# Rescaling of 64-bit weights on GpSimd without the absolute value, and the squares of that stage on ScalarE

## The chip, the cores and the metric

One core of one Trainium2 chip. The metric is the device time of one launch in microseconds; the kernel before has a median of 714.84 us over three runs (712.4 to 716.45).

## The reference

Three layers follow each other. Attention between 4 x 8 sequences of 512 rows and 32 state rows, both ways; a dense layer of 512 x 2048 x 512 on the resulting 2176 tokens with g = h * tanh(softplus(h)); a layer of 8 experts, of which each token takes the one with the largest similarity.

```python
scores = scale * np.matmul(x, state.transpose(0, 1, 3, 2))
a = np.exp(scores - scores.max(-1, keepdims=True)); a /= a.sum(-1, keepdims=True) + 1e-09
xread = np.matmul(a, state)
...
h = x @ w_in
sp = np.where(h > 20.0, h, np.log1p(np.exp(np.minimum(h, 20.0))))
g = h * np.tanh(sp)
return (g @ w_out).astype(np.float32)
```

The weights `w_in` and `w_out` arrive as 64-bit floats, seen by the kernel as pairs of 32-bit words.

## The kernel before

**Conversion.** The two weights are 32 tiles of 128 x 512 (16 of `w_in`, 16 of `w_out`; `order0`, line 197: the first 8 of each, then the second 8). `load_w` loads one raw tile of 512 KB into one of two buffers (`raw`); `convert_w` calls `convert` (line 87) on it. The high word, read as a 32-bit float and rescaled, has the wanted exponent three bits too low: line 96 rescales it with an absolute value on ScalarE into `x`, line 99 makes three more mantissa bits of the low word on GpSimd, and VectorE puts them together in two instructions (lines 100 and 101, both recorded at line 70): shift left by three and or, then or with the sign bit of the raw tile. The second of them frees the raw buffer for the next load. `split` (line 72) then makes a rounded copy on ScalarE (line 73, `wih`, `woh`) and the rest on GpSimd (line 74, `wil`, `wol`). Names carry the tile: `wc05x` is tile 5 of `w_in`, `wc115x` tile 15 of `w_out`.

**Steps.** The dense layer runs in steps (chunk of 512 tokens, slice of 128 of the 2048 hidden values), listed in `steps` from `RUNS`: steps 0 to 7 are slices 0 to 7 of chunk 0, steps 8 to 23 slices 0 to 15 of chunk 1. `l1` makes the hidden slice in PSUM (`h`), `mish_a` (line 508) makes tanh and silu of it on ScalarE (lines 513 and 514, the start of a step there) and squares the tanh in `z` (tile `er`): line 517 on ScalarE or line 519 on VectorE. `mish_b` makes two more squares on ScalarE (lines 542, 543) and two products on VectorE (line 70). `g_split` splits the result (`gh` on ScalarE, `gl` on VectorE), and `l2` multiplies it with `w_out`, two steps later. In the first 24 steps (`NCONV`) each step also calls `convert_w` at its end.

**Attention.** Ahead of the steps, eight units go through four phases; GpSimd subtracts the maximum (line 372) and applies the reciprocal sum (line 387). The first 8 conversions are called among them, two more before step 2; steps 0 and 1 begin during its last units.

**What sets the order.** Outside the last chunk the order of instructions on each engine is made at build time by a scheduler with its own model of costs, so a change of one instruction's engine can move its neighbours too. Each engine then executes its list in order.

Of the kernel before, what the change touches and what calls it, by code (L numbers as in the profile page):

```python
# [8 lines left out]
F32 = mybir.dt.float32  # L9
# [6 lines left out]
ALU = mybir.AluOpType  # L16
AF = mybir.ActivationFunctionType
# [20 lines left out]
NCONV = 24  # L38
# [13 lines left out]
def body(tc, x, state, w_in, w_out, ee, tau, w1, w2, out):  # L52
    nc = tc.nc
    T, V, A, G, Y = nc.tensor, nc.vector, nc.scalar, nc.gpsimd, nc.sync
# [14 lines left out]
    def stt(o, a, s, b, op0, op1):  # L69
        V.scalar_tensor_tensor(out=o, in0=a, scalar=s, in1=b, op0=op0, op1=op1)  # L70

    def split(hi, lo, src, eng=None):
        A.activation(hi, src, AF.Copy)  # L73
        (eng or V).tensor_tensor(out=lo, in0=src, in1=hi.bitcast(F32), op=ALU.subtract)  # L74
# [12 lines left out]
    def convert(pl, hi, lo, raw, name, bufs):  # L87

        if not wide:
            split(hi, lo, raw[:, 0:512], G)  # L90
            return
        low, top = raw[:, :, 0], raw[:, :, 1]
        x = pl.tile([P, 512], U32, tag="cx", name=name + "x", bufs=bufs)
        xf = x.bitcast(F32)

        A.activation(xf, top.bitcast(F32), AF.Abs, scale=2.0**-112)

        l16 = raw.rearrange("p a b -> p (a b)").bitcast(U16).rearrange("p (a b) -> p a b", b=4)[:, :, 1]
        G.tensor_scalar(out=low, in0=l16, scalar1=2.0**-13, scalar2=-0.49994, op0=ALU.mult, op1=ALU.add)
        stt(x, x, 3, low, ALU.logical_shift_left, ALU.bitwise_or)  # L100
        stt(x, top, 0x80000000, x, ALU.bitwise_and, ALU.bitwise_or)
        split(hi, lo, xf, G)
# [6 lines left out]
    with stack:  # L109
# [82 lines left out]
        def pair(name):  # L192
            t = mt.tile([P, 2, 512], F32, tag="er", bufs=2, name=name)
            return t[:, 0, :], t[:, 1, :]
# [14 lines left out]
        def convert_w():  # L209
            o, i = j = order.pop(0)  # L210
            if o:
                hi, lo = (w[i // 2][:, i % 2, :] for w in (WOH, WOL))
            else:
                g, k = divmod(i, KT)
                hi, lo = (w[g // 2][k][:, g % 2 * 512 : (g % 2 + 1) * 512] for w in (WIH, WIL))
            convert(cv, hi, lo, raws.pop(j), f"wc{o}{i}", 2)
            load_w()
# [290 lines left out]
        def mish_a(c, f):  # L508

            z, _ = pair(f"er{c}_{f}")  # L510
            u = mt.tile([P, 512], F32, tag="u", bufs=2, name=f"u{c}_{f}")
            h = hps.pop((c, f))
            A.activation(z, h, AF.Tanh, scale=0.5, bias=mb_[:, 0:1])  # L513
            A.activation(u, h, AF.Silu)  # L514

            if steps.index((c, f)) < NCONV and f % 2:
                A.activation(z, z, AF.Square)
            else:
                V.tensor_tensor(out=z, in0=z, in1=z, op=ALU.mult)  # L519

            nrm[c, f] = u, z, h
# [532 lines left out]
        steps = [(c, f) for c, a, b in RUNS for f in range(a, b)]  # L1054
# [43 lines left out]
        def start(g):  # L1098
            l1(*steps[g])
            following(*steps[g])  # L1100
            mish_a(*steps[g])
            if g:
                finish(g - 1)
            mish_b(*steps[g])
# [66 lines left out]
        for g, (c, f) in enumerate(steps):  # L1171
# [32 lines left out]
            if at == 2 and r:  # L1204
                pc, pf, _ = RUNS[r - 1]
                evac(pc, pf)
                if 1 < r < len(RUNS) - 2:
                    todo += [ab(pc, i) for i in range(CHUNKS[pc][1] + 2)]
            mish_a(c, f)
            if c != LC or f:  # L1210
                finish(g - 1)
# [113 lines left out]
```

## Time and profile before

| | |
|---|---|
| median of three runs | 714.84 us (712.4 to 716.45) |
| the profiled execution | 714.88 us, of which the span is 713.0 us |
| mean granted TensorE clock | 0.987 of full |
| busy: TensorE, VectorE, ScalarE, GpSimd | 670.7, 479.5, 453.4, 188.1 us |

Rows below are of that execution; times in them count from the start of the span. PE is TensorE, PEld its weight loads, DVE VectorE, ACT ScalarE, POOL GpSimd, SP SyncE. L96 is line 96 of the kernel before.

### The profile page before, as it was taken

The numbers are of one execution on the slowest core, as the hardware profiler recorded it, in microseconds if no ns is written. First come the engines' busy times: TensorE is split into PE (matmuls) and PEld (weight loads), VectorE is DVE, ScalarE is ACT, GpSimd is POOL, SyncE is SP. The second block draws the span as 40 slices with busy tenths as digits, with TensorE's granted clock in tenths as the row PEclk, the third lists the DMA queues.
The fourth block names the chain that finished last, engine by engine and source line by source line (L and its number), as shares of the span: only waits on it lengthen the run. The fifth ranks groups of instructions, "written<-read, shape, count | busy, mean of one in ns | idle before, by whom it ended". The sixth has DMA issues, their size and how long they took to land.

```text
span 713.0 us, 11919 instructions
## 1 busy us (share of the span) xinstructions
PE 670.7 (94%) x3517; PEld 550.4 (77%) x3517; DVE 479.5 (67%) x1002; ACT 453.4 (64%) x798; POOL 188.1 (26%) x166
## 2 busy tenths in 40 slices
PE   8888998999999999999999889999999999999894
PEld 8788876778888888888887768877876788777673
DVE  5977798989477776776679687673345751347751
ACT  5876989989798677677776687314334641246640
POOL 2785355562000030210030454021211211121101
PEclk9999999999999999999999989999999999999997
DMA  7662143430010454422021656014416641257440
GB/s 196 151 172 90 60 127 110 148 118 31 1 60 0 123 112 99 89 56 86 29 75 61 207 192 213 10 60 148 161 50 221 220 133 61 95 205 242 190 136 18
DMA packets 57829, 81.23 MB, mean 114 GB/s; under 512 B 24970, under 2 KB 35722, under 8 KB 57748
## 3 DMA queue, kind: packets, MB, share of 16 engines
q1 hardware_dynamic: 54388, 70.31, 32.5%
q0 software_dynamic: 3360, 9.99, 4.3%
q8 instruction: 33, 0.54, 0.3%
q14 instruction: 48, 0.39, 0.2%
HBM read 64.00 MB, written 13.65 MB: 109 GB/s over the span
## 4 chain that ended last, share of the span: by engine, by line
PE 42%; issue 24%; DMA 13%; ACT 9%; DVE 8%; POOL 3%; SPq 0%; POOLq 0%; DVEq 0%; ACTq 0%
DMA out<-ys,ix 8%; PE acc L105 6%; PE acc L106 6%; PE acc L107 6%; PE h L105 3%; PE h L106 3%; PE h L107 3%; DMA es<-in_moe_w 2%; PE lg L599 2%; DMA w<-in_moe_w_out 2%; DMA w<-in_moe_w_in 1%; ACT er L513 1%; PE x1t L588 1%; PE hp L107 1%; PE hp L106 1%
## 5 line engine op out<-in xcount | busy, mean ns | idle before, releaser
L105 PE MATMUL acc<-woh,gh 128*128 128x512 f32 x272 | 109.8, 407 | 5.5 <-ACT gh L73 5.5
L106 PE MATMUL acc<-wol,gh 128*128 128x512 f32 x272 | 108.3, 399 | 0.0
L107 PE MATMUL acc<-woh,gl 128*128 128x512 f32 x272 | 94.2, 402 | 1.0 <-DVE gl L74 0.9
L1051 POOL DMA_INDIRECT out<-ys,ix x21 | 21.2, 1011 | 203.4 <-DVEq L1048 108.8
L105 PEld LDWEIGHTS acc<-woh,gh 128*128 128x128 f32 x272 | 51.8, 191 | 18.8 <-ACT gh L73 8.6
L107 PEld LDWEIGHTS acc<-woh,gl 128*128 128x128 f32 x272 | 51.0, 190 | 14.5 <-DVE gl L74 3.3
L513 ACT ACTIVATE er<-h,mb__104 128x512 f32<-128x512 f32 x68 | 46.8, 688 | 23.8 <-PE h L107 21.6
L106 PEld LDWEIGHTS acc<-wol,gh 128*128 128x128 f32 x272 | 51.8, 190 | 10.3
L985 PE MATMUL y<-w2h,hth 128*128 128x512 f32 x136 | 55.9, 411 | 2.8 <-DVE htl L74 1.1
L519 DVE TENSOR_TENSOR er<-er 128x512 f32<-128x512 f32 x56 | 41.3, 737 | 23.1 <-ACT er L513 22.7
L985 PE MATMUL hp<-w1h,xth 128*128 128x512 f32 x136 | 55.3, 407 | 0.8 <-PE ht L1020 0.2
L986 PE MATMUL y<-w2l,hth 128*128 128x512 f32 x136 | 55.2, 406 | 0.1
L986 PE MATMUL hp<-w1l,xth 128*128 128x512 f32 x136 | 53.8, 395 | 0.0
L105 PE MATMUL h<-xh,mh 128*128 128x512 f32 x128 | 52.0, 406 | 0.5 <-ACT xh L73 0.5
L542 ACT ACTIVATE h<-er,mb__104 128x512 f32<-128x512 f32 x68 | 47.4, 697 | 7.3 <-DVE er L519 4.9
L106 PE MATMUL h<-xl,mh 128*128 128x512 f32 x128 | 50.9, 397 | 0.4 <-DVE xl L74 0.4
L107 PE MATMUL h<-xh,ml 128*128 128x512 f32 x128 | 50.5, 395 | 0.0
L543 ACT ACTIVATE er<-er,mb__104 128x512 f32<-128x512 f32 x68 | 49.5, 727 | 1.2
L73 ACT ACTIVATE xth<-gt 128x512 fp32r<-128x512 f32 (+1 forms) x21 | 11.4, 543 | 57.7 <-PE gt L965 57.7
L73 ACT ACTIVATE hth<-ht 128x512 fp32r<-128x512 f32 x32 | 17.5, 595 | 42.3 <-PE ht L1020 40.9
L62 DVE TENSOR_SCALAR ys<-y,gt 128x512 f32<-128x512 f32 x21 | 15.7, 748 | 39.1 <-PE y L990 32.1
L514 ACT ACTIVATE u<-h 128x512 f32<-128x512 f32 x68 | 40.6, 597 | 0.0
(456 smaller groups left out, 1717.6 us busy)
## 6 DMA issues: line engine op xcount, KB each, us to landing
sg<-in_moe_w SPq DMA_DIRECT2D x48, 512.0 KB, 5.2
w<-in_moe_w_in SPq DMA_DIRECT2D x16, 512.0 KB, 4.1
w<-in_moe_w_out SPq DMA_DIRECT2D x16, 512.0 KB, 3.3
es<-in_moe_w SPq DMA_DIRECT2D x32, 256.0 KB, 3.0
xn<-in_x SPq DMA_DIRECT2D x32, 128.0 KB, 3.4
md<-mr SPq DMA_DIRECT2D x28, 128.0 KB, 2.5
x1d<-x SPq DMA_DIRECT2D x13, 256.0 KB, 3.2
mh<-mr SPq DMA_DIRECT2D x28, 64.0 KB, 2.1
```

The costliest lines, as they stand in the source:

```text
L73: A.activation(hi, src, AF.Copy)
L105: T.matmul(o, lh, rh, start=first, stop=False)
L106: T.matmul(o, lh, rl, start=False, stop=False)
L107: T.matmul(o, ll, rh, start=False, stop=last)
L513: A.activation(z, h, AF.Tanh, scale=0.5, bias=mb_[:, 0:1])
L514: A.activation(u, h, AF.Silu)
L519: V.tensor_tensor(out=z, in0=z, in1=z, op=ALU.mult)
L542: A.activation(r, z, AF.Square, scale=QS, bias=mb_[:, 1:2])
L543: A.activation(z, z, AF.Square, scale=QS, bias=mb_[:, 2:3])
L985: T.matmul(o, h, wh, start=k == 0, stop=False)
L986: T.matmul(o, h, wl, start=False, stop=k == len(terms) - 1)
L1051: G.indirect_dma_start(out=out[:, :], out_offset=bass.IndirectOffsetOnAxis(ap=ix, axis=0), in_=y, in_offset=None, bounds_check=NTOK - 1, o ...
```

## The change

Line 96 goes from ScalarE to GpSimd as a plain multiplication that keeps the sign; the shift left by three in the next instruction drops the sign bit together with two exponent bits, so the absolute value is not needed. In the first 24 steps the square of every step is done on ScalarE (line 517), where before the even slices had theirs on VectorE (line 519).

```diff
-        A.activation(xf, top.bitcast(F32), AF.Abs, scale=2.0**-112)
+        G.tensor_scalar(out=xf, in0=top.bitcast(F32), scalar1=2.0**-112, scalar2=None, op0=ALU.mult)
...
-            if steps.index((c, f)) < NCONV and f % 2:
+            if steps.index((c, f)) < NCONV:
                 A.activation(z, z, AF.Square)
             else:
                 V.tensor_tensor(out=z, in0=z, in1=z, op=ALU.mult)
```

The order on the engines moves at more places than these. On GpSimd, at the end of the attention stage, before (`w_...` is a raw tile, `a_...` a unit's weights):

```order
L372 TENSOR_TENSOR a_876<-ss_789,mx_874 128x512
L74 TENSOR_TENSOR wil_178<-wc07x,wih_170 128x512
L99 TENSOR_SCALAR w_988<-w_988 128x512
L99 TENSOR_SCALAR w_1122<-w_1122 128x512
L387 TENSOR_TENSOR a_876<-a_876,sm_890 128x512
L372 TENSOR_TENSOR a_934<-ss_872,mx_932 128x512
L99 TENSOR_SCALAR w_1131<-w_1131 128x512
L387 TENSOR_TENSOR a_934<-a_934,sm_948 128x512
```

And with the change:

```order
L372 TENSOR_TENSOR a_934<-ss_872,mx_932 128x512
L387 TENSOR_TENSOR a_876<-a_876,sm_890 128x512
L96 TENSOR_SCALAR wc07x<-w_847 128x512
L74 TENSOR_TENSOR wil_177<-wc06x,wih_169 128x512
L99 TENSOR_SCALAR w_930<-w_930 128x512
L387 TENSOR_TENSOR a_934<-a_934,sm_948 128x512
L96 TENSOR_SCALAR wc10x<-w_930 128x512
L74 TENSOR_TENSOR wil_178<-wc07x,wih_170 128x512
L99 TENSOR_SCALAR w_988<-w_988 128x512
L96 TENSOR_SCALAR wc11x<-w_988 128x512
L99 TENSOR_SCALAR w_1122<-w_1122 128x512
```

Three of line 99 (`w_988`, `w_1122`, `w_1131`) and one split moved behind the last unit's line 387.

On VectorE, at the end of the conversion, before (`h_9` is slice 9 of chunk 1, step 17):

```order
L74 TENSOR_TENSOR gl_8_1933<-h_8_1850,gh_8_1932 128x512
L70 SCALAR_TENSOR_TENSOR wc115x<-wc115x,w_2149 128x512
L70 SCALAR_TENSOR_TENSOR wc115x<-w_2149,wc115x 128x512
L70 SCALAR_TENSOR_TENSOR h_9_1908<-h_9_1908,u_9_1928 128x512
L519 TENSOR_TENSOR er_10_1985<-er_10_1985 128x512
```

And with the change:

```order
L74 TENSOR_TENSOR gl_10_2032<-h_10_1949,gh_10_2031 128x512
L70 SCALAR_TENSOR_TENSOR wc115x<-wc115x,w_2149 128x512
L70 SCALAR_TENSOR_TENSOR wc115x<-w_2149,wc115x 128x512
L70 SCALAR_TENSOR_TENSOR h_11_2007<-h_11_2007,u_11_2027 128x512
L70 SCALAR_TENSOR_TENSOR h_11_2007<-er_11_2026,h_11_2007 128x512
```

The last conversion stands two steps later, and line 519 is gone from these steps.

## Rows read from the trace of the kernel before

**Rows 1.** The page, part 1: busy time of each engine.

```profile
PE 670.7 (94%) x3517; PEld 550.4 (77%) x3517; DVE 479.5 (67%) x1002; ACT 453.4 (64%) x798; POOL 188.1 (26%) x166
```

**Rows 2.** Windows by stage: us, busy time and instructions by engine, clock, DMA.

```profile
16.00:62.00 46.00, 37.97 (x327) 36.03 (x328) 40.77 (x98) 35.06 (x72) 35.00 (x30) 1.00 0.57 162
...
100.00:166.00 66.00, 60.95 (x286) 47.26 (x285) 59.31 (x84) 60.42 (x110) 37.61 (x34) 1.00 0.39 125
166.00:200.00 34.00, 34.00 (x160) 28.05 (x159) 21.72 (x34) 26.45 (x46) 3.10 (x3) 1.00 0.00 1
...
78.94:174.47 95.53, 90.48 (x427) 71.80 (x426) 86.08 (x124) 88.25 (x161) 51.86 (x45) 1.00 0.35 111
```

**Rows 3.** Timeline of ACT, line 513, steps 2, 18, 20, 21: start, duration.

```profile
78.94 0.67 ACT L513 ACTIVATE er<-h,mb__104 128x512 f32<-128x512 f32 x1
...
165.26 0.72 ACT L513 ACTIVATE er<-h,mb__104 128x512 f32<-128x512 f32 x1
...
174.47 0.69 ACT L513 ACTIVATE er<-h,mb__104 128x512 f32<-128x512 f32 x1 [0.25 <-PE h L107]
178.66 0.69 ACT L513 ACTIVATE er<-h,mb__104 128x512 f32<-128x512 f32 x1 [1.19 <-PE h L107]
```

**Rows 4.** Waits, 100 to 165 us: total, times, longest.

```profile
PEld acc L105 <- ACT gh L73: 6.6, 7, 2.2
POOL w L99 <- DMA w<-in_moe_w_in: 6.4, 5, 1.7
POOL w L99 <- DMA w<-in_moe_w_out: 5.4, 5, 1.2
...
PE acc L105 <- ACT gh L73: 3.9, 5, 1.7
```

**Rows 5.** Timeline of ACT: conversions 12 and 32, and instructions with their followers.

```profile
80.67 0.68 ACT L96 ACTIVATE wc12x<-w 128x512 f32<-128x512 f32 x1
...
119.44 0.63 ACT L517 ACTIVATE er<-er 128x512 f32<-128x512 f32 x1
119.96 1.09 ACT L557 ACTIVATE part<-acc 128x512 f32<-128x512 f32 x2
120.91 0.68 ACT L96 ACTIVATE wc012x<-w 128x512 f32<-128x512 f32 x1
121.46 0.71 ACT L542 ACTIVATE h<-er,mb__104 128x512 f32<-128x512 f32 x1
...
163.56 0.71 ACT L96 ACTIVATE wc115x<-w 128x512 f32<-128x512 f32 x1
```

**Rows 6.** Groups by line: minimum, median, maximum ns; L542 of 60 to 200 us.

```profile
L519 DVE TENSOR_TENSOR er<-er x56: 660/692/1361, 69.4 to 428.7; 128x512 f32<-128x512 f32 x56
L99 POOL TENSOR_SCALAR w<-w x32: 643/667/1171, 17.2 to 163.5; 128x512 uint32<-128x512 uint16 x32
L387 POOL TENSOR_TENSOR a<-a,sm x8: 1047/1048/1552, 16.1 to 67.8; 128x512 f32<-128x512 f32 x8
L74 POOL TENSOR_TENSOR wil<-wc00x,wih x1: 1267/1267/1267, 21.7 to 21.7; 128x512 fp32r<-128x512 f32 x1
...
L542 ACT ACTIVATE h<-er,mb__104 128x512 f32<-128x512 f32 x25 | 17.4, 698 | 1.4 <-DVE er L519 1.1
```

**Rows 7.** Timeline of POOL, the last attention products.

```profile
62.84 0.78 POOL L99 TENSOR_SCALAR w<-w 128x512 uint32<-128x512 uint16 x1 [2.60 <-DMA w<-in_moe_w_out]
...
66.65 0.65 POOL L99 TENSOR_SCALAR w<-w 128x512 uint32<-128x512 uint16 x1 [0.89 <-DMA w<-in_moe_w_out]
67.78 1.05 POOL L387 TENSOR_TENSOR a<-a,sm 128x512 f32<-128x512 f32 x1 [0.48 <-DVE sm L386]
```

**Rows 8.** Timelines of POOL and DVE beside each other, and one group.

```profile
28.72 0.69 DVE L70 SCALAR_TENSOR_TENSOR wc02x<-wc02x,w 128x512 uint32<-128x512 uint32 x1
28.76 1.55 POOL L387 TENSOR_TENSOR a<-a,sm 128x512 f32<-128x512 f32 x1
...
46.06 0.68 DVE L369 TENSOR_REDUCE mx<-ss 128x16 f32<-128x512 f32 x1
46.66 0.68 DVE L70 SCALAR_TENSOR_TENSOR wc05x<-w,wc05x 128x512 uint32<-128x512 uint32 x1
48.21 1.71 POOL L74 TENSOR_TENSOR wil<-wc05x,wih 128x512 fp32r<-128x512 f32 x1
48.83 1.65 DVE L70 SCALAR_TENSOR_TENSOR wc06x<-w,wc06x 128x512 uint32<-128x512 uint32 x1
...
103.92 1.17 DVE L70 SCALAR_TENSOR_TENSOR wc08x<-w,wc08x 128x512 uint32<-128x512 uint32 x1
...
165.25 1.67 DVE L70 SCALAR_TENSOR_TENSOR wc115x<-w,wc115x 128x512 uint32<-128x512 uint32 x1
...
L70 DVE SCALAR_TENSOR_TENSOR h<-h,u x24: 681/690/700, 72.4 to 193.0; 128x512 f32<-128x512 f32 x24
```

## The prediction

> **What bounds the kernel now.** I read the page's busy shares first: TensorE is busy for 94% of the span [rows 1], so only the places where it is not matter. The windows by stage show two such places. From 166 to 200 us, with no weights left to convert, TensorE is busy all the time; from 100 to 166 us, in the middle of the conversion, it is busy for 60.95 of 66.00 us, ScalarE for 60.42, VectorE for 59.31 and GpSimd for 37.61 [rows 2]. The granted clock is 1.00 in all of them, so the clock plays no part.
>
> The busy share hides part of the slack. Line 513 starts each step on ScalarE, so its starts are the step's pace: 165.26 to 178.66 us is three steps, 4.47 us each, with TensorE full; step 2 starts at 78.94 us and step 18 at 165.26 us, which is 5.40 us each [rows 3]. I take steps 2 to 20, 78.94 to 174.47 us, as the stretch that the change can touch: 95.53 us for 18 steps that TensorE alone would do in 18 x 4.47 = 80.5 us. ScalarE is busy for 88.25 us of it (92%), VectorE for 86.08 (90%) [rows 2]. The waits of 100 to 165 us say the same: TensorE's and its weight loads' largest ones are for `gh`, ScalarE's split of the activated tile [rows 4]. The stretch is bound by ScalarE with VectorE close behind, not by TensorE.
>
> **Part 1: ScalarE.** 22 of the 32 conversions lie in the stretch; line 96 runs from 80.67 to 163.56 us [rows 5]. Each costs ScalarE the distance to its next instruction, 0.55 us (120.91 to 121.46) [rows 5]: 22 x 0.55 = 12.1 us go. In come the squares of the 9 even steps 2 to 18, at 0.52 us each (119.44 to 119.96 [rows 5]): 4.7 us. ScalarE falls from 88.25 to 80.9 us. Both functions run among the same neighbours before and after, and the order shows no further table load; I cost that at nothing. The square also no longer goes from ScalarE to VectorE and back; ScalarE waited 1.1 us for that from 60 to 200 us [rows 6], too little to count.
>
> **Part 2: VectorE.** It loses 9 squares. Of a row with a 692 ns median [rows 6] I count 0.60 us each, since back-to-back instructions start 0.60 us apart (46.06 to 46.66 [rows 8]): 5.4 us, 86.08 to 80.7. What it may get back is a hold-up by GpSimd. A GpSimd split starts at 48.21 and takes 1.71 us; the conversion's second VectorE instruction starts at 48.83 and takes 1.65 us instead of 0.68. The other way round, VectorE's instruction at 28.72 makes the GpSimd one at 28.76 take 1.55 us instead of 1.05 [rows 8]. From 100 to 166 us, 14 of VectorE's instructions are over 0.79 us, the first and last of them in [rows 8]; their excess over 0.69 is 7.6 us for 37.61 us of GpSimd work [rows 2], 0.20 us per us.
>
> The added GpSimd instruction has no row. It is nearest to line 99, one input of as many elements on that engine, median 667 ns; the bounds are that row's minimum, 643 ns, and the two-input ones, 1.05 and 1.27 us [rows 6]. I take 0.667 us. So 22 x 0.667 = 14.7 us of new GpSimd work there, and 14.7 x 0.20 = 3.0 us of hold-up: VectorE ends at 83.7 us. Between nothing and the full 14.7 us I stay with the measured rate, since the new instruction comes before its own tile's VectorE work and can only meet another tile's.
>
> **Part 3: the sum of the stretch.** Today's fullest engine, ScalarE, fills 92.4%. Afterwards VectorE is the fullest with 83.7 us; at the same fill that is 90.6 us, so **4.9 us** less. TensorE's 80.5 and ScalarE's 80.9 lie below that. GpSimd has 51.86 us of work [rows 2]; 66.6 with the new instructions, still far from full. Its waits for a load (6.4 and 5.4 us [rows 4]) are on the instruction that stands beside the new one, so no new wait arises there, but the splits queued behind start 0.667 us later. They are needed steps later.
>
> **Part 4: the attention stage, up to 69 us.** Ten of the moved instructions belong to it, and GpSimd is busy for 35.00 of the 46 us from 16 to 62 [rows 2]. But the scheduler moves conversions back. Ahead of the last attention product on GpSimd (line 387, at 67.78 us) stand 12 of line 99 and 8 splits before; now 9 of line 99, 8 of line 96 and 7 splits: 5 x 0.667 more and one 1.27 less, 2.0 us more work. Two line 99's that stood there waiting for loads, 2.60 and 0.89 us [rows 7], now stand behind it. 2.0 - 3.5 = -1.5; VectorE has three tiles fewer ahead of its last sum, and the same three to catch up in steps 0 to 2. I take **1 us** gained. Bounds: 3.5 us gained (the waits go, the work is hidden), 8 x 0.667 = 5.3 us lost (all of it on the path). SyncE's order changes by two small loads that move ahead of weight loads: nothing, as each of these loads is issued when a buffer comes free, not when the queue is.
>
> **Sum.** The profiled execution took 714.9 us (the median of the three is 714.84, so no correction): 714.9 - 4.9 - 1.0 = **709.0 us**. What is gained is kept, because from 166 us on TensorE is full and simply starts earlier.
>
> **The rivals.**
>
> *Full hold-up, slower.* VectorE's conversion instructions read two tiles from SBUF, and such an instruction and a GpSimd one wait for each other to end; the one with an input in PSUM (`h<-h,u`, 24 times) never exceeds 700 ns [rows 8]. If each new instruction holds VectorE for its whole 0.667 us, VectorE needs 80.7 + 14.7 = 95.4 us, at 92.4% fill 103.2: 7.7 us more, and with the 1 us of part 4 the time is 714.9 + 7.7 - 1.0 = **721.6 us**. It decides from where VectorE is as full as ScalarE is now: (88.25 - 80.7) / 22 = 0.34 us of hold-up per conversion, against 0.14 in my sum. Against it: today's rate. For it: the long ones come mostly in exactly these instructions. The Trainium skill, "SBUF — State Buffer", "Who interferes with whom", states this as an exclusive lock: a VectorE instruction with two SBUF inputs and a GpSimd instruction that reads SBUF block each other for the whole instruction. By that rule the trace agrees on what meets (1.65 us against 0.68), and by the rule alone the price per meeting is a whole instruction; how often they meet only the row tells; the 721.6 us is the case of a meeting at every tile.
>
> *The load loop, no change.* Two buffers hold the raw tiles; a load waits for VectorE's second conversion instruction, and GpSimd waits for the load nearly every time [rows 4]. 22 conversions from 80.67 to 163.56 us are 21 intervals, 10.5 rounds of 7.9 us. Before, rescaling on ScalarE ran beside line 99; now it follows it. If every round grows by 0.667 us, the conversions take 7.0 us longer. The last of them stands two steps later in the order, worth 2 x 4.47 = 8.9 us, so 1.9 us remain: 714.9 - 1.9 = **713.0 us**.
>
> *TensorE-bound, faster still.* If ScalarE and VectorE no longer wait for each other, the stretch falls to VectorE's 83.7 us, 11.8 us less: 714.9 - 11.8 - 1.0 = **702.1 us**. Against it: in order, each engine still waits for the others.
>
> **Chances.** Differences under 0.5%, 3.6 us, can't be told from no change here. My forecast gets 0.45; the load loop 0.25 (same); the full hold-up 0.20 (slower); the TensorE-bound case 0.10. Faster 0.55, same 0.25, slower 0.20. The range leaves out the far half of the two outer cases: from 704 (2.5 us more from part 4 and a third of the way to the TensorE-bound case) to 718 us (the hold-up at half its price: 714.9 + 3.9 - 1.0).
>
> **What would show it.** Right: the new GpSimd instruction near 0.67 us; steps 2 to 20 in about 90.6 us; ScalarE under 90% there; VectorE's instructions over 0.79 us about as frequent as now; the last line 387 before 68 us. Full hold-up: VectorE over 95% busy and most conversion instructions at 1.2 us and more. Load loop: ScalarE and VectorE both waiting for GpSimd, which waits for loads, and rounds over 8.4 us. I am wrong if the attention stage ends after 70 us, or if the new instruction takes over 1 us.

## The result and the profile after

The changed kernel takes 723.01 us (median of three runs; 722.99 to 723.52) against 715.05 us for the kernel before on the same chip: a ratio of 1.0108, 95% interval 1.0077 to 1.0138. It is **slower** by 1.1%, 14 us above the forecast of 709.0 and outside the range of 704 to 718. (One further run of 2316.92 us was disturbed and is left out.) The profiled execution took 723.52 us.

First the page, part 1, of the kernel after, to be held against [rows 1]:

```profile
PE 675.8 (94%) x3517; PEld 557.1 (77%) x3517; DVE 488.3 (68%) x990; ACT 442.4 (61%) x778; POOL 237.6 (33%) x198
```

ScalarE lost 11 us of work, as meant. GpSimd gained 49.5 us for 32 new instructions, 1.55 us each, and VectorE, which lost work, became busier by 8.8 us. The groups of the new instruction, a usual one and the longest (minimum, median, maximum ns):

```profile
L96 POOL TENSOR_SCALAR wc12x<-w x1: 1523/1523/1523, 83.1 to 83.1; 128x512 f32<-128x512 f32 x1
...
L96 POOL TENSOR_SCALAR wc17x<-w x1: 2012/2012/2012, 105.0 to 105.0; 128x512 f32<-128x512 f32 x1
```

The windows after, for [rows 2]: the attention stage, and steps 2 to 20, which now run from 81.39 to 184.49 us:

```profile
16.00:62.00 46.00, 41.61 (x353) 40.91 (x353) 41.59 (x97) 30.18 (x64) 40.24 (x35) 0.93 0.53 133
...
81.39:184.49 103.10, 95.14 (x440) 76.54 (x439) 90.34 (x113) 81.39 (x148) 85.53 (x67) 0.97 0.31 103
```

And line 513 on ScalarE, steps 0, 1, 2 and 20, for [rows 3]:

```profile
65.69 0.69 ACT L513 ACTIVATE er<-h,mb__104 128x512 f32<-128x512 f32 x1
...
77.68 0.69 ACT L513 ACTIVATE er<-h,mb__104 128x512 f32<-128x512 f32 x1 [2.80 <-PE h L107]
...
81.39 0.69 ACT L513 ACTIVATE er<-h,mb__104 128x512 f32<-128x512 f32 x1
...
184.49 0.67 ACT L513 ACTIVATE er<-h,mb__104 128x512 f32<-128x512 f32 x1
```

Step 2 begins 2.45 us later than in [rows 3], and steps 2 to 20 take 103.10 us instead of 95.53, 7.57 more: step 20 is 10.0 us late, of which the end (723.52 against 714.88) gets 1.4 us back. So the whole loss arises before step 20. No engine is full in that stretch: VectorE is busy for 90.34 of 103.10 us (88%), ScalarE for 81.39 (79%), and TensorE's 95.14 (92%) are a smaller share than the 95% of before. The granted clock is lower in this execution (0.93 and 0.97 in the two windows, 1.00 in [rows 2]; mean 0.978), but it is not what costs the time: the two other runs had a mean of 0.984 and 0.986, nearly the 0.987 of before, and took 723.0 us.

What the engines then wait for, 78 to 190 us (total, times, longest). The kernel before has three waits of ScalarE for a converted tile, these:

```profile
ACT woh L73 <- DVE wc15x L70: 0.8, 1, 0.8
ACT woh L73 <- DVE wc111x L70: 0.4, 1, 0.4
ACT wih L73 <- DVE wc013x L70: 0.3, 1, 0.3
```

The kernel after has 15, 15.4 us in all, here the first four, and TensorE's wait that follows from them:

```profile
PE acc L105 <- ACT gh L73: 7.9, 4, 3.3
...
ACT wih L73 <- DVE wc08x L70: 4.2, 1, 4.2
ACT wih L73 <- DVE wc012x L70: 2.2, 1, 2.2
...
ACT woh L73 <- DVE wc112x L70: 1.4, 1, 1.4
ACT wih L73 <- DVE wc010x L70: 1.4, 1, 1.4
```

ScalarE's time was freed and then spent waiting for VectorE's converted tiles. The longest of these waits, in ScalarE's timeline (start, duration, instruction, idle before it):

```profile
111.88 0.73 ACT L543 ACTIVATE er<-er,mb__104 128x512 f32<-128x512 f32 x1
116.85 0.63 ACT L73 ACTIVATE wih<-wc08x 128x512 fp32r<-128x512 f32 x1 [4.24 <-DVE wc08x L70]
117.52 0.60 ACT L73 ACTIVATE gh<-h 128x512 fp32r<-128x512 f32 x1
```

`gh`, for which TensorE waits, stands right behind in ScalarE's list. Why tiles are late shows on the two engines in front. This one had first waited 2.80 us for its load; of the next ones two waited 0.75 and 0.66 us, and are late all the same. GpSimd's timeline of the kernel after:

```profile
111.05 0.67 POOL L99 TENSOR_SCALAR w<-w 128x512 uint32<-128x512 uint16 x1 [2.80 <-DMA w<-in_moe_w_in]
...
117.41 1.51 POOL L96 TENSOR_SCALAR wc09x<-w 128x512 f32<-128x512 f32 x1
118.89 1.28 POOL L74 TENSOR_TENSOR wil<-wc08x,wih 128x512 fp32r<-128x512 f32 x1
120.93 1.07 POOL L99 TENSOR_SCALAR w<-w 128x512 uint32<-128x512 uint16 x1 [0.75 <-DMA w<-in_moe_w_in]
122.08 1.54 POOL L96 TENSOR_SCALAR wc010x<-w 128x512 f32<-128x512 f32 x1
123.59 1.30 POOL L74 TENSOR_TENSOR wil<-wc09x,wih 128x512 fp32r<-128x512 f32 x1
125.55 1.13 POOL L99 TENSOR_SCALAR w<-w 128x512 uint32<-128x512 uint16 x1 [0.66 <-DMA w<-in_moe_w_in]
126.76 1.53 POOL L96 TENSOR_SCALAR wc011x<-w 128x512 f32<-128x512 f32 x1
128.25 1.28 POOL L74 TENSOR_TENSOR wil<-wc010x,wih 128x512 fp32r<-128x512 f32 x1
```

VectorE's timeline beside it:

```profile
118.96 1.77 DVE L70 SCALAR_TENSOR_TENSOR wc09x<-wc09x,w 128x512 uint32<-128x512 uint32 x1
120.77 0.69 DVE L70 SCALAR_TENSOR_TENSOR wc09x<-w,wc09x 128x512 uint32<-128x512 uint32 x1
...
123.65 1.79 DVE L70 SCALAR_TENSOR_TENSOR wc010x<-wc010x,w 128x512 uint32<-128x512 uint32 x1
...
128.32 1.76 DVE L70 SCALAR_TENSOR_TENSOR wc011x<-wc011x,w 128x512 uint32<-128x512 uint32 x1 [0.15 <-POOL wc011x L96]
...
130.60 0.82 DVE L70 SCALAR_TENSOR_TENSOR wc011x<-w,wc011x 128x512 uint32<-128x512 uint32 x1
```

Line 96 ends at 118.92, 123.62 and 128.29 us and releases VectorE's first conversion instruction. GpSimd's next instruction is the split of the tile before; it starts at the same moment, 1.3 us long, and VectorE's takes 1.77 us instead of 0.69. Of the 22 conversions in the steps, 17 have a first instruction over 1.2 us, mean 1.45; before, it was 3 of 22, mean 0.86 (both counted over the timeline of VectorE).

These lines are also a round of the two raw buffers: a raw tile goes into the buffer that the tile two before it leaves, so a round is two conversions. SyncE's issues of the loads of tiles 11 and 13 of `w_in` in the kernel after:

```profile
121.52 0.33 SPq L83 DMA_DIRECT2D w<-in_moe_w_in  x1
...
131.49 0.33 SPq L83 DMA_DIRECT2D w<-in_moe_w_in  x1
```

VectorE's second instruction is done with the buffer of tile 9 at 121.46 us, and the load of tile 11 into it is issued at 121.52. Line 99 takes the tile up at 125.55, line 96 ends at 128.29, VectorE's second instruction at 131.42, and the next load is issued at 131.49: 9.97 us, in which only the load, GpSimd and VectorE follow each other. Before, with line 96 on ScalarE beside line 99, such a round could be far shorter: that of tile 15 took 6.34 us, from its load's issue at 127.94 to the next at 134.28, less than the mean of 7.89. GpSimd's and VectorE's timelines before have it so:

```profile
132.00 0.68 POOL L99 TENSOR_SCALAR w<-w 128x512 uint32<-128x512 uint16 x1 [1.57 <-DMA w<-in_moe_w_in]
...
132.72 0.69 DVE L70 SCALAR_TENSOR_TENSOR wc015x<-wc015x,w 128x512 uint32<-128x512 uint32 x1 [0.40 <-POOL w L99]
133.44 0.69 DVE L70 SCALAR_TENSOR_TENSOR wc015x<-w,wc015x 128x512 uint32<-128x512 uint32 x1
```

Over the 22 conversions, the 11th to the 32nd, line 96 now runs from 83.10 to 181.56 us, 10.5 rounds of 9.38 us instead of 7.89. That is 15.6 us more; the last conversion stands two steps later in the order, and two steps at 4.47 us are 8.9, so 6.7 us are left, most of the 7.57. The chain of work followed back from the start of step 20, made as in part 4 of the page, says the same: of the stretch 25.4 us lie on these loads, 28.5 on GpSimd, 27.6 on VectorE, 10.7 on ScalarE and nothing on TensorE; before it was 12.6, 5.7, 19.4, 37.2 and 14.3 us. The steps now wait for the conversions, and these for the round through the buffers.

### The profile page after: what moved, and what is told of

Its sections match the earlier page's. It is cut to its first block, busy times and chain, and to the rows that moved or that the text cites. A ratio compares the mean times of both kernels' runs of the same rounds, so it can differ in the third digit from the quotient of the medians.

```text
span 721.7 us, 11853 instructions
## 1 busy us (share of the span) xinstructions
PE 675.8 (94%) x3517; PEld 557.1 (77%) x3517; DVE 488.3 (68%) x990; ACT 442.4 (61%) x778; POOL 237.6 (33%) x198
## 5 line engine op out<-in xcount | busy, mean ns | idle before, releaser
L107 PE MATMUL acc<-woh,gl 128*128 128x512 f32 x272 | 96.5, 404 | 1.4 <-DVE gl L74 1.4
L542 ACT ACTIVATE h<-er,mb__104 128x512 f32<-128x512 f32 x68 | 47.2, 695 | 7.0 <-DVE er L519 4.2
L519 DVE TENSOR_TENSOR er<-er 128x512 f32<-128x512 f32 x44 | 32.6, 740 | 19.5 <-ACT er L513 19.0
```

The source lines that it names most:

```text
L107: T.matmul(o, ll, rh, start=False, stop=last)
L542: A.activation(r, z, AF.Square, scale=QS, bias=mb_[:, 1:2])
```

## The experiments

The first runs were to tell whether the rescaling or the squares cost the time, the later ones whether it is the length of the new instruction or what it meets. Each ratio is to the kernel before on the same chip; the first four below shared a chip, then the next four, then the last four. None of the kernels leaves out a part of the computation.

**The two halves apart.** The squares alone, without the rescaling:

```diff
-            if steps.index((c, f)) < NCONV and f % 2:
+            if steps.index((c, f)) < NCONV:
```

> The rescaling stays on ScalarE with its absolute value; every square of the first 24 steps goes to ScalarE. Theory A (the new GpSimd instruction is what costs, by its length and by what it holds up): this half alone gives a small gain or nothing, 711 to 715 us. Theory B (the squares overload ScalarE): slower than before by 3 us or more, 718 to 723 us.

Measured: 717.14 us, ratio 1.0019 [1.0000, 1.0038], between what the two theories gave. ScalarE waits for converted tiles 1.8 us in all (here and below from 78 to 190 us). And the rescaling alone:

```diff
-        A.activation(xf, top.bitcast(F32), AF.Abs, scale=2.0**-112)
+        G.tensor_scalar(out=xf, in0=top.bitcast(F32), scalar1=2.0**-112, scalar2=None, op0=ALU.mult)
```

> The rescaling goes to GpSimd; the squares stay split as before. Theory A: as slow as the whole change or slower, 722 to 728 us, with the new instruction at 1.5 us and more and the first VectorE instruction of most conversions at 1.7 us. Theory B: as before, 713 to 717 us.

Measured: 723.80 us, ratio 1.0115 [1.0081, 1.0148]; ScalarE's waits for converted tiles 14.1 us. The rescaling carries the whole loss; the squares gain nothing, alone or on top of it.

**What the instruction costs.** Eight forms, written ahead of the attention stage, each twice; the first of each, up to 15 us, ran while GpSimd had no other work, most of the second ones among that of the attention stage:

```diff
+            kw = dict(op0=ALU.mult)
+            for i in range(2):
+                G.tensor_scalar(out=outs[i], in0=src[:, 0:512], scalar1=2.0**-112, scalar2=None, **kw)
+                G.tensor_scalar(out=outs[i], in0=odd, scalar1=2.0**-112, scalar2=None, **kw)
...
+                G.tensor_scalar(out=outs[i], in0=odd, scalar1=2.0**-112, scalar2=0.0, op0=ALU.mult, op1=ALU.add)
...
+                G.tensor_tensor(out=outs[i], in0=odd, in1=half_[:, 0:1].to_broadcast([P, 512]), op=ALU.mult)
+                G.tensor_copy(outs[i], odd)
```

> The kernel before with sixteen extra GpSimd instructions in the attention stage that write a tile not yet in use (its time is not of interest). They differ in one thing each: 32-bit float input contiguous or every second element, scalar 2 to the minus 112 or 0.5, one or two operations, 16-bit input, output every second element, two tensors, plain copy. If the stride costs, only the strided ones take 1.5 us; if the 32-bit float input costs, all float ones do and the 16-bit ones take 0.67 us; if the tiny scalar costs, 0.5 is faster; if one operation is slower than two (a slower path), the two-operation one takes 0.67 us.

The groups of that kernel; line 353 is one operation on neighbouring elements, 354 on every second one, 356 two operations on every second one, 359 two tensors, 360 a copy:

```profile
L353 POOL TENSOR_SCALAR at<-at x2: 1492/1517/1542, 3.9 to 12.2; 128x512 f32<-128x512 f32 x2
...
L354 POOL TENSOR_SCALAR at<-at x2: 1523/1550/1577, 5.5 to 15.3; 128x512 f32<-128x512 f32 x2
...
L356 POOL TENSOR_SCALAR at<-at x2: 658/659/660, 8.8 to 29.6; 128x512 f32<-128x512 f32 x2
...
L359 POOL TENSOR_TENSOR at<-at,half__110 x2: 1042/1200/1358, 11.1 to 36.0; 128x512 f32<-128x512 f32 x2
L360 POOL COPY at<-at x2: 649/650/652, 14.6 to 40.9; 128x512 f32<-128x512 f32 x2
```

With one operation the instruction takes 1.52 us, with two 0.66: the stride does not matter, the number of operations does. (With 0.5 as the scalar, line 355, one operation took 1.52 and 1.54 us.) Line 99, from which the forecast took its 0.667, has two. The kernel's own time (725.33, with the probes in it) is of no interest.

**The whole change with a shorter instruction**, as a product of two tensors and as two operations:

```diff
-        G.tensor_scalar(out=xf, in0=top.bitcast(F32), scalar1=2.0**-112, scalar2=None, op0=ALU.mult)
+        G.tensor_tensor(out=xf, in0=top.bitcast(F32), in1=resc.to_broadcast([P, 512]), op=ALU.mult)
```

> The whole change, but the rescaling on GpSimd is a multiplication of two tensors, the second one column read 512 times. Such an instruction took 1.05 us in the attention stage. If the length of the instruction is what costs, 0.5 us less of it for 32 conversions gives back 3 to 8 us: 715 to 720 us. If only its place in the queue and the order made by the scheduler cost, nothing changes: 721 to 725 us.

Measured: 719.88 us, ratio 1.0048 [1.0025, 1.0071]; line 96 took 1.04 to 1.49 us. In its profiled execution (720.68 us) step 20 begins 13.2 us later than before and the end comes 5.8 us later, so lateness at step 20 does not carry to the end one for one.

```diff
-        G.tensor_scalar(out=xf, in0=top.bitcast(F32), scalar1=2.0**-112, scalar2=None, op0=ALU.mult)
+        G.tensor_scalar(out=xf, in0=top.bitcast(F32), scalar1=2.0**-112, scalar2=0.0, op0=ALU.mult, op1=ALU.add)
```

> The whole change, but the rescaling on GpSimd is written as two operations, times 2 to the minus 112 plus 0.0, the form that took 0.66 us in the probes against 1.52 for one operation. That is the length which the prediction assumed. Theory A (the length of the new instruction, and what it makes VectorE and ScalarE wait, is the whole loss): 709 to 714 us, faster than before or the same. Theory C (the loss is in the chain itself: GpSimd's two instructions in a row ahead of VectorE's, and the split right behind them that holds VectorE, whatever the length): 716 to 721 us.

Measured: 720.05 us, ratio 1.0066 [1.0044, 1.0088]. The price accounts for about 3 us of the nearly 8 (1.0108 - 1.0066 of 715; the two intervals overlap): at the very price of the forecast the change is still slower. ScalarE waits 15.4 us for converted tiles, as long as with the long form. With the squares left as before:

> The rescaling on GpSimd in the two-operation form, the squares split as before. Theory A: 711 to 716 us. Theory C: 717 to 722 us. Against the run with both parts it says what the squares give when ScalarE has been relieved.

Measured: 719.77 us, ratio 1.0046 [1.0020, 1.0072], within the interval of the run above it: again nothing from the squares. Against the rescaling alone in its long form (1.0115) this pair puts the price at 5 us.

**GpSimd's time alone.** The kernel before, with a one-operation instruction added behind each split on the finished rest, so that VectorE's part of the conversion does not wait for it:

```diff
-        split(hi, lo, xf, G)
+        split(hi, lo, xf, G); G.tensor_scalar(out=lo, in0=lo.bitcast(F32), scalar1=1.0, scalar2=None, op0=ALU.mult)
```

> The kernel before, with one more GpSimd instruction of the slow one-operation form for each conversion: it multiplies the finished rest of the weight tile by 1.0 in place, so nothing in the conversion waits for it. If GpSimd's load and the hold-up of VectorE make the loss, this alone costs 4 us or more: 720 to 726 us. If the loss comes from VectorE waiting for the rescaled tile, the same work off that path costs little: 715 to 719 us.

Measured: 721.53 us, ratio 1.0063 [1.0036, 1.0090]. The loss lies elsewhere than the change's: step 2 begins at 87.17 us, 8.2 late, and steps 2 to 20 take 96.7, 1.2 us more than before. On GpSimd's timeline of this kernel:

```profile
67.64 1.81 POOL L102 TENSOR_SCALAR wil<-wil 128x512 fp32r<-128x512 f32 x1
...
70.39 1.49 POOL L102 TENSOR_SCALAR wil<-wil 128x512 fp32r<-128x512 f32 x1
72.59 1.05 POOL L387 TENSOR_TENSOR a<-a,sm 128x512 f32<-128x512 f32 x1 [0.71 <-DVE sm L386]
```

The last attention product, at 67.78 us in [rows 7], comes at 72.59, behind two of the added instructions. What it waited for last, 0.71 us, was VectorE's `sm`, and that stood behind the square of step 0 in VectorE's list; so how much of the 8.2 us is GpSimd's time and how much the order stays open. The steps lost nearly nothing by it.

**Where the split stands.** The two-operation form with the split's rest on VectorE, so that no split stands behind line 96 on GpSimd:

```diff
-        split(hi, lo, xf, G)
+        split(hi, lo, xf, V)
```

> As the whole change with the two-operation form, and the rest of each converted weight tile (the split that stands behind the rescaling on GpSimd) goes to VectorE. GpSimd then has two instructions of 0.66 us for each conversion and no split that could hold VectorE's first instruction. Theory C: faster than the two-operation run by 2 us or more, though VectorE gets 32 x 0.6 us more work. Theory A: slower than it by 2 us or more, since VectorE was the fullest engine by the prediction's sum.

Measured: 716.82 us, ratio 1.0016 [0.9991, 1.0042]. Steps 2 to 20 take 92.2 us, 3.3 less than before, but step 2 begins at 83.41, 4.5 us late. So in the next kernels the ten conversions ahead of step 2 stay as before, and only the 22 of the steps change. First with the split left on GpSimd, then with it on VectorE for those 22:

```diff
-        G.tensor_scalar(out=xf, in0=top.bitcast(F32), scalar1=2.0**-112, scalar2=None, op0=ALU.mult)
+        (G.tensor_scalar(out=xf, in0=top.bitcast(F32), scalar1=2.0**-112, scalar2=0.0, op0=ALU.mult, op1=ALU.add)) if late else A.activation(xf, top.bitcast(F32), AF.Abs, scale=2.0**-112)
...
-        split(hi, lo, xf, G)
+        split(hi, lo, xf, V if late else G)
...
-            convert(cv, hi, lo, raws.pop(j), f"wc{o}{i}", 2)
+            convert(cv, hi, lo, raws.pop(j), f"wc{o}{i}", 2, len(order) < len(order0) - 10)
```

> The first ten conversions as in the kernel before, the other 22 with the two-operation rescaling on GpSimd and the rest left on GpSimd; all squares on ScalarE. It differs from the run with the rest on VectorE in nothing else. If the split right behind the rescaling, which holds VectorE's first instruction, is what is left of the loss: steps 2 to 20 in 98 to 101 us, 717 to 720 us. If not: 709 to 713 us.

Measured: 722.66 us, ratio 1.0071 [1.0044, 1.0097]; its profiled execution, from which the rows below are, took 727.05, the longest of its seven.

> The first ten conversions (the attention stage's) as in the kernel before; the other 22 with the two-operation rescaling on GpSimd and their rest on VectorE; all squares of the first 24 steps on ScalarE. With both changes everywhere, steps 2 to 20 took 92.2 us against 95.5, but step 2 began 4.5 us late. If these two are independent, the start is that of the kernel before and the gain stays: 709 to 713 us. If the attention stage's delay is hidden anyway or the steps were fast only because the weights came earlier, 714 to 717 us.

Measured: 715.85 us, ratio 0.9990 [0.9969, 1.0011]. In the code these two differ in nothing but the engine of the split's rest in the steps (the order follows from it), and they differ by 5.8 us by the two ratios (6.8 between the medians). GpSimd's timeline of the slower one:

```profile
120.09 0.65 POOL L96 TENSOR_SCALAR wc011x<-w 128x512 f32<-128x512 f32 x1
120.70 1.28 POOL L74 TENSOR_TENSOR wil<-wc010x,wih 128x512 fp32r<-128x512 f32 x1
```

VectorE's timeline of the slower one:

```profile
120.77 1.76 DVE L70 SCALAR_TENSOR_TENSOR wc011x<-wc011x,w 128x512 uint32<-128x512 uint32 x1 [1.28 <-POOL wc011x L96]
```

And VectorE's timeline of the faster one, the same tile:

```profile
120.94 0.69 DVE L70 SCALAR_TENSOR_TENSOR wc011x<-wc011x,w 128x512 uint32<-128x512 uint32 x1
121.55 0.69 DVE L74 TENSOR_TENSOR wil<-wc010x,wih 128x512 fp32r<-128x512 f32 x1
```

With the split behind it line 96 takes 0.65 us, and VectorE's instruction is still held for the split. Of the 44 conversion instructions 22 are over 0.79 us in the one and 7 in the other (24 in the change, 17 before); of the 22 first ones, 7 and none are over 1.2 us. ScalarE waits for converted tiles 16.2 us in the one and 7.6 in the other. What in the split's place counts is not shown. It ends the meeting, it takes work off GpSimd (though as much of it, added off VectorE's path, cost the steps only 1.2 us in the kernel with the added instruction), and the order is another: the faster one has its last conversion one step later on VectorE, worth 4.47 us by the sum above, while the rounds are almost alike (8.27 and 8.12 us). The gain that was hoped for did not come, though: the faster one equals the kernel before. VectorE now does the rests, and step 2 begins at 82.02 us; why 3 us later than before, with the same ten conversions ahead of it, stays open (the order differs there). The same kernel with the squares as before:

> The same with the squares split between VectorE and ScalarE as before. If VectorE is the fuller engine once it has the 22 rests, this is slower than the run with all squares on ScalarE by 1 to 4 us; if the engines' load does not decide, equal.

Measured: 716.59 us, ratio 0.9999 [0.9983, 1.0016]. No version beat the kernel before.

**The attention stage's share.** The one-operation form as in the change, but in the 22 conversions of the steps alone:

> The same as the last with the one-operation form, so the change itself confined to the 22 conversions of the steps. Against the whole change it says what the ten conversions of the attention stage cost: if the loss lies in the steps, as its timeline has it (step 2 began 2.5 us late, steps 2 to 20 took 103.1 us against 95.5), 720 to 723 us; if the attention stage carries most of it, 715 to 718 us.

Measured: 719.42 us, ratio 1.0049 [1.0027, 1.0070], against 1.0108 for the change, between the two cases expected. So about 0.6%, 4 us, come from moving the first ten conversions, and about 0.5% from the other 22. By the traces the 4 us do not lie in the attention stage alone: step 2 begins 1.0 us earlier than in the change, and steps 2 to 20 take 100.63 us, 2.5 less. With the short form the shares are others: 1.0066 for all 32 and 1.0071 for the 22 alone, so there the ten cost nothing. The 22 cost no less with the short instruction (1.0071 against 1.0049, intervals that overlap), though the long one has 18 of the 22 first instructions over 1.2 us and the short one 7: the count of meetings alone does not rank these two. What is left of the loss with the short form stays open.

## Why the prediction was wrong

**What bounds the kernel: half right.** The waits for `gh` were the right place. But "the fullest engine's fill" was a poor model: it says that a lighter ScalarE helps, and the chain from load to GpSimd to VectorE to ScalarE's copy became longer, from 7.9 to 9.4 us for a round of two tiles.

**Part 1, ScalarE: right in size, worth nothing.** 80.9 us were forecast for the stretch and 81.39 measured. The 6.9 us went into waits: 1.5 us for converted tiles before, 15.4 after.

**Part 2, VectorE: this step failed,** in both factors. The price of the new instruction was taken from line 99, 0.667 us; it is 1.51 to 2.01 us, above even the upper bound of 1.27. In the stretch that is 85.53 - 51.86 = 33.7 us of GpSimd work, not 14.7. And the rate: "can only meet another tile's" overlooked what stands behind the instruction on GpSimd. Releasing VectorE at the end of line 96 starts both engines at once, so the next split meets the released instruction in most tiles, 17 of 22. VectorE came to 90.34 us; 90.34 - 80.7 = 9.6 us of hold-up for 33.7 us, 0.29 per us against the 0.20 taken over from before. Per conversion that is 0.44 us, beyond the 0.34 from which the slower rival was to decide. The runs say what each is worth: the price 3 to 5 us of the loss, and the split's place 5.8 us at the low price, by whichever of its effects.

**Part 3, the stretch: this step failed too.** 90.6 us forecast, 103.10 measured. Even with VectorE's true 90.34 us, the same fill of 92.4% would give 97.8; the other 5 us have no full engine behind them. "So no new wait arises there" was the mistake: GpSimd's waits for a load are 16.0 us from 78 to 190 us, against 14.4 before, and in each round line 96 and the hold-up of VectorE now come on top, one after the other. The round, not the fullest engine, sets the time of the stretch. With the two-operation form the rounds take 8.12 us and the waits for a load 15.0 us (7.0 at line 99, 8.0 at line 96, which comes first for some tiles); the steps are 4.9 us longer than before all the same, of which 10.5 x (8.12 - 7.89) = 2.4 us are the rounds' and the rest is unexplained.

**Part 4, the attention stage: wrong in sign.** 1 us of gain forecast, 2.45 us of loss at step 2. The last line 387 came at 67.11 us, before the 67.78 of [rows 7], and step 0 at 65.69 us, 3.0 us earlier than before. But step 1 began at 77.68 instead of 74.47. TensorE's timeline after shows a stop between the two, at `m`, a product of the state rows with `w_in`; the last unit's transposes stand right behind it there, at 71.23 us:

```profile
70.06 0.38 PE L105 MATMUL m<-wih,STh 128*128 128x256 f32 x1 [2.89 <-DVE ml L74]
```

VectorE's timeline after has that `ml` behind a held conversion of tile 7, and waiting for ScalarE's `mh`:

```profile
67.60 1.42 DVE L70 SCALAR_TENSOR_TENSOR wc07x<-w,wc07x 128x512 uint32<-128x512 uint32 x1
69.32 0.69 DVE L74 TENSOR_TENSOR ml<-m,mh 128x512 fp32r<-128x512 f32 x1 [0.30 <-ACT mh L73]
```

And ScalarE's timeline after has the start of step 0, with its table loads, ahead of `mh`:

```profile
66.39 1.28 ACT L514 ACT_TABLE_LOAD   x1
...
68.70 0.59 ACT L73 ACTIVATE mh<-m 128x512 fp32r<-128x512 f32 x1
```

So step 0 came early at the expense of the last unit: the order was another one, and the prediction, which counted GpSimd's queue ahead of line 387 alone, could not see that. The tiles that it let VectorE catch up at no price came late, too: tile 7 of `w_in` is finished at 69.0 us, before at 56.2, and the last of the ten at 78.1, before at 63.1. How much of the 2.45 us is the order's and how much GpSimd's stays open: step 2 begins at 81.03 us with the squares alone and at 80.38 with the conversions of this stage as before. What the runs show is the 0.6% between the change and the run with the 22 conversions alone. Of its two signs of being wrong, one (the new instruction over 1 us) came; for the other (the attention stage ending after 70 us) the last line 387, on which the prediction looked, was the wrong thing to watch.

**The squares: right** that they matter little: 4.7 us of work moved, and a ratio of 1.0019 [1.0000, 1.0038].

**The rivals.** The full hold-up came nearest with 721.6 us and had a chance of 0.20. Its stretch of 103.2 us is what was measured (103.10), but by luck, not by its sum: VectorE was to be over 95% busy and was 88%; the time is a chain of waits, not a full engine. The Trainium skill, "SBUF — State Buffer", "Who interferes with whom", says that a VectorE instruction with two inputs in SBUF contends with a GpSimd instruction that reads SBUF, by an exclusive lock; the traces agree (1.76 us against 0.69 on the same tile), and by that rule alone the hold-up at every tile was to be feared. How often they meet is set by the order on the queues, and there the forecast trusted the old rate. The load loop, with a chance of 0.25, was right in its mechanism and wrong in its price: its signs came (rounds of 9.38 us, over its 8.4; ScalarE's waits for VectorE's tiles 15.4 us, VectorE's for GpSimd 6.1 against 1.6 before, both from 78 to 190 us). It allowed 0.667 us more per round, 7.0 us in all, which the later place of the last conversion would have paid for; the rounds grew by 1.49 us, 15.6 in all, and 6.7 us were left unpaid. The TensorE-bound case did not come.

## What to carry to other kernels

Price an added instruction by its exact form, number of operations included, not by a neighbour with the same shape. When an instruction moves to another engine, look at what stands right behind it there: the engine that it releases starts at the same moment as that neighbour, so if the two hold each other up, they meet far more often than an average rate from before says. Add up the round through the buffers as well as the busy times: an instruction that moves from beside that round into it lengthens every round, and no engine has to be full for that. And relieving a nearly full engine is worth nothing when the relief only makes it wait for the chain that feeds it.

## What was not expected of the hardware

On GpSimd a multiplication of 128x512 f32 by a scalar takes 1.52 us as one operation and 0.66 us with an added "plus 0.0"; a copy takes 0.65, a product of two tensors 1.04 (1.36 among the work of the attention stage). In the kernel the long form took up to 2.01 us beside VectorE. Neither the stride nor the value of the scalar makes the difference; why one operation takes longer than two stays open.
